# A spectral mixer gated with attention: first weights loaded in two halves on two queues, other warm-up products, and a later slot for one set of reciprocals

## The chip, the cores and the metric

The kernel runs on one core of a Trainium2 chip. A core has five instruction queues that run side by side: TensorE (PE), VectorE (DVE), ScalarE (ACT), GpSimd (POOL) and SyncE (SP), which here only issues DMA transfers. PE multiplies from SBUF into PSUM, which has eight banks of 128 x 512 fp32. The metric is device time in microseconds of one execution, as the median of several runs.

## What is computed

Two branches share the input x (2048 tokens, 512 channels, fp32), and a gate for each token mixes them.

```python
g = sigmoid((x * gate_w).sum(-1, keepdims=True))
a = einsum("ts,bse->bte", dft_seq_re, x @ dft_hid_re.T) - einsum("ts,bse->bte", dft_seq_im, x @ dft_hid_im.T)
q, k, v = split(x @ wqkv)                 # 32 heads of 16
b = (softmax(q @ k.T * 16 ** -0.5) @ v) @ wo
out = g * a + (1 - g) * b
```

## The kernel before, in words

Every fp32 operand of a large product is split into a high and a low part (fp32r); three products (high x high, high x low, low x high) accumulate in one PSUM bank.

**The start.** `staged_first` (lines 103 to 108) loads the first two tiles of 256 KB, x from ACT's queue and the first weights from SP's. `warm_up` (143 to 155) clears a tile of zeros with two memsets on DVE, then gives PE four products of 128 x 128 and seven of 128 x 512 on the zeros while the loads are under way. The fourth small product releases the other loads (line 97). `split_first` (127 to 141) casts both halves of the weights on ACT (line 136) and x on DVE (137), and then forms the low parts. The first real products are those of line 220: for each 128 rows of the contraction they need the high part of x and, product by product, one quarter of the columns of the weights.

**The main loop.** The attention walks through 512 units: 16 pairs of heads, two halves of the queries, 16 tiles of keys. For each unit PE computes scores (line 740), ACT takes the exponential (741), and PE multiplies with the values (762, in the last 16 units 748); the values carry a column of ones, so that each softmax sum comes out beside its output. Ahead of that run products whose only use is the row maxima (262); DVE reduces them (264). When the maxima of half a pair are complete, DVE, POOL and DVE turn them into rows (273, 276 and 277, 281), and DMAs place these rows beside the queries (287), where the scores pick them up. The Fourier part and the projection with `wo` (429) are woven in between by a pattern written out by hand (`segment`, `pairs`). `run_plan(u)` sets off, at the start of a slot, all steps with a due unit u; the engines then take what they got in the order of the program.

**Outputs of the attention.** The results of each half of the queries (hf 0 or 1) and of each group of four pairs (ct 0 to 3) go to DRAM. `sums` (line 531) loads the softmax sums from there as a 128 x 64 tile, `inverse` takes the reciprocals on DVE (536) and writes them to DRAM (539), and `load_o` reads outputs (554) and reciprocals, repeated for 16 rows (556), into tiles of one shape, which are multiplied and split for the projection. The last group of the second half (hf 1, ct 3) has only three pairs, so its transfers go pair by pair, six and six, and its tile is cleared first on POOL (547). Its steps are those of `last_block`: at unit 486 load outputs and reciprocals together, at 490 multiply on POOL (592), at 494 split on DVE (578, 579) into `o_lno` and `o_lnh`. Its sums are loaded at 482 and inverted at 484. For the first half (hf 0, ct 3) the same steps come later, at 498 to 506, with a step "sums" of its own for the reciprocals.

**The last 20 units.** From unit 492 on, two units make one slot: four scores, some products of the projection (line 429, dealt out by the table `whole`), four scores, sixteen products with the values. `third` is the projection of the second half's last group; its first three products stand in the slot of unit 496 and read `o_lno`. `last` is the projection of the first half's last group, in the slots 508 and 510; its banks rotate through the pools psS, psA, psD (the list `three`). psS and psA have three banks each and are shared with the scores; psD has one. The projections' banks are read out on DVE (615).

The tile framework gives each DMA of SP and ACT one of eight semaphores in turn, so a DMA also waits until the one eight places before it has landed.

Of the kernel before, what the change touches and what calls it, by code (L numbers as in the profile page):

```python
# [9 lines left out]
F32 = mybir.dt.float32  # L10
# [5 lines left out]
P = 128  # L16
S = 2048
D = 512
# [13 lines left out]
def mix_kernel(ctx: ExitStack, tc: tile.TileContext, xa_t, xa, wqkv, w_hid, w_seq, wo, gate_w, out):  # L32
# [5 lines left out]
    nc = tc.nc  # L38
# [64 lines left out]
    def staged_first(w, x):  # L103

        w_raw, x_raw = (st1.tile([P, D], F32, name="raw", bufs=RAW) for _ in range(2))
        nc.scalar.dma_start(x_raw, x)
        nc.sync.dma_start(w_raw, w)
        return w_raw, x_raw

    def add(hi, lo, src, lo_eng, shape=None):  # L110
# [16 lines left out]
    def split_first():  # L127

        (wh0, wl0, w, _, _), (xh0, xl0, x, _, _) = todo.pop(0), todo.pop(0)
        w_raw, x_raw = staged_first(w, x)  # L130
        behind.append(warm_up())
        load_ahead(RAW - 3)
        x_raw = x_raw.rearrange("p (s t) -> p s t", s=4)
        halves = [slice(i * D // 2, (i + 1) * D // 2) for i in range(2)]
        for cols in halves:
            nc.scalar.copy(wh0[:, cols], w_raw[:, cols])
        nc.vector.tensor_copy(xh0, x_raw)
        for cols in halves:
            nc.vector.tensor_tensor(wl0[:, cols], w_raw[:, cols], wh0[:, cols].bitcast(F32), ALU.subtract)
        nc.vector.tensor_tensor(xl0, x_raw, xh0.bitcast(F32), ALU.subtract)  # L140
        load_ahead()

    def warm_up():

        zeros = xab[3][:, 0, 0]
        nc.vector.memset(zeros[:, :P].bitcast(F32), 0.0)
        nc.vector.memset(zeros[:, P:].bitcast(F32), 0.0)
        make_identity(nc, ident)
        nc.vector.tensor_tensor(pairsum, ident[:, :64], ident[:, 64:], ALU.add)
        ps = psD.tile([P, 512], F32, name="d")  # L150
        for i in range(4):
            first = nc.tensor.matmul(ps[:, :P], zeros[:, :P], zeros[:, :P], start=True, stop=True)
        for i in range(7):
            nc.tensor.matmul(ps, zeros[:, :P], zeros, start=True, stop=True)
        return first

    def add_x(tb, kt):
        x = xab[tb][:, :, :, kt * P:(kt + 1) * P]
# [4 lines left out]
    def bank():  # L163
        nonlocal banks
        banks += 1
        return (psS if banks % 2 else psA).tile([P, 512], F32, name="s" if banks % 2 else "a")


    with tc.tile_pool(name="qk", bufs=1, reuse_waits="tile") as pool:
# [38 lines left out]
        for tb in range(4):  # L208
# [4 lines left out]
            for c in range(2):  # L213
                if tb == 0 and c == 0:
                    pss = [bank() for _ in range(4)]
                    for kt in range(KT):
                        x = xab[tb][:, :, :, kt * P:(kt + 1) * P]
                        for i, (w, v) in enumerate(((wh, 0), (wl, 0), (wh, 1))):
                            for ct in range(4):
                                nc.tensor.matmul(pss[ct], w[:, c, kt, ct * P:(ct + 1) * P], x[:, :, v],  # L220
                                                 start=kt == 0 and i == 0, stop=kt == KT - 1 and i == 2)
# [4 lines left out]
                for ct in range(4):  # L226
                    ps = bank()
# [143 lines left out]
    for s in range(8):  # L371
        ps = psS.tile([P, 512], F32, name="s")
# [128 lines left out]
    def place(i, dt, name):  # L501

        return const.tile([P, 2, 2, 2 * D], dt, name=name, tag=f"xab{i}")

    def tiles(t):
        return [[t[:, v, q * P:(q + 1) * P] for v in range(2)] for q in range(t.shape[2] // P)]
# [34 lines left out]
    def load_o(o, sm, hf, ct, q0, n=4):  # L541

        size = (sm if o is None else o).shape[1]
        cols = slice(q0, q0 + size)
        for t in (o, sm):
            if n < 4 and t is not None:
                nc.gpsimd.memset(t, 0.0)
        for h in range(2):
            o0 = 33 if h else 0
            for p in [slice(0, 4)] if n == 4 else [slice(i, i + 1) for i in range(n)]:  # L550
                r = slice(64 * h, 64 * h + 64) if n == 4 else slice(64 * h + p.start, 64 * h + 64, 4)
                rows = o_d[hf][4 * ct + p.start:4 * ct + p.stop, o0:o0 + 16, cols]
                if o is not None:
                    nc.sync.dma_start(o[r], rows.rearrange("p d f -> d p f"))
                if sm is not None:
                    nc.sync.dma_start(sm[r], r_d[hf][ct][h:h + 1, p, cols].broadcast_to([16, p.stop - p.start, size]))
# [20 lines left out]
    def parts(hi, lo, src):  # L577
        nc.vector.tensor_copy(hi, src)
        nc.vector.tensor_tensor(lo, src, hi.bitcast(F32), ALU.subtract)

    def last_block(step, hf, n, eng):

        if step == 0:
            if not last_o:
                last_o.append(place(1, F32, "o_raw"))
            t = last_o[0][:, hf]
            load_o(t[:, 0], t[:, 1] if hf else None, hf, 3, 0, n)
        elif step == "sums":
            load_o(None, last_o[0][:, hf, 1], hf, 3, 0, n)
        elif step == 1:  # L590
            t = last_o[0][:, hf]
            eng.tensor_tensor(t[:, 0], t[:, 0], t[:, 1], ALU.mult)
        else:
            o = last_o[0][:, hf, 0]
            if hf:
                ts = [work.tile([P, 2, D], F32R, name=f"o_l{x}", tag=x) for x in ("no", "nh")]
                for i, t in enumerate(ts):
                    parts(t[:, 0], t[:, 1], o[:, i * D:(i + 1) * D])
                oh[hf, 3] = tiles(ts[0]) + tiles(ts[1])
            else:  # L600
                t = place(2, F32R, "o_l")[:, 0]
                parts(t[:, 0], t[:, 1], o)
                oh[hf, 3] = tiles(t)
# [13 lines left out]
    def proj(hf, cts, pools, qts=range(8)):  # L617

        for qt in qts:
            t = hf * 8 + qt  # L620
            chain = Chain(*pools[qt % len(pools)], 3 * len(cts))
            for ct in cts:
                h1, l1 = oh[hf, ct][qt]
                for i, (st, mv) in enumerate(((h1, 0), (h1, 1), (l1, 0))):
                    last = ct == cts[-1] and i == 2
                    yield chain, st, wos[0][:, mv, ct], partial(proj_next, hf, cts, t, chain) if last else None
# [174 lines left out]
    def at(u, f, *args):  # L801
        plan.setdefault(u, []).append(partial(f, *args))

    for hf in range(2):
        for ct in range(4):
            n = 3 if hf and ct == 3 else 4
            last = 32 * (4 * ct + n - 1) + 16 * (hf + 1)
            at(last + (4 if ct < 3 else 2), sums, hf, ct, n)
            at(last + (12 if ct < 3 else 4), inverse, hf, ct, n)
            if ct < 3:  # L810
                for half in range(2):
                    for step, du in enumerate((16, 20, 22)):
                        at(last + du + 8 * half, block, step, hf, ct, half)
# [3 lines left out]
    one, two, three = [(psD, "d")], [(psS, "s"), (psD, "d")], [(psS, "s"), (psA, "a"), (psD, "d")]  # L817
    at(456, load_yg, 0, range(3))
    at(481, load_yg, 0, range(3, 8))
    for step, u in enumerate((486, 490, 494)):  # L820
        at(u, last_block, step, 1, 3, nc.gpsimd)
    for step, u in ((0, 498), ("sums", 500), (1, 504), (2, 506)):
        at(u, last_block, step, 0, 4, nc.gpsimd)
    at(498, load_w15)
    lead = a_next

# [75 lines left out]
    first = proj(0, (0, 1, 2), one * 5 + two[:1] + one, range(7))  # L902
# [22 lines left out]
    run_deferred()  # L925
    assert not any(a_left.values())
    third = proj(1, (3,), two)
    last = proj(0, (3,), three, range(7))

    early, late = proj(0, (0,), one, (7,)), proj(0, (1, 2, 3), [(psS, "s")], (7,))  # L930
    whole = {492: ((first, 9),), 494: ((first, 6),), 496: ((first, 3), (third, 3)), 498: ((third, 6),), 500: ((third, 6),),
# [55 lines left out]
```

## Time and profile before

| | |
|---|---|
| median of 3 runs | 1707.89 us (1707.83 to 1707.91) |
| the profiled execution | 1708.24 us, of which its span from the first to the last instruction is 1706.4 us |
| granted TensorE clock, mean | 0.999 |
| PE busy | 1698.9 us in 13042 matmuls |
| DVE busy | 1353.1 us (79%) |
| ACT busy | 1152.2 us (68%) |
| POOL busy | 450.1 us (26%) |
| DMA | 165.09 MB, 97 GB/s on average |

A row of the timeline has the start in microseconds from the first instruction, the busy time, the engine, the line of the kernel, the operation, the tile written and the tiles read, the shape, and how many instructions were merged into the row. In square brackets stands how long the engine had been idle before it, and what ended that. SPq and ACTq are the queues that issue DMAs; their time is that of issuing, not of the transfer. A row of the waits has the engine, tile and line that waited, what it waited for, the sum in microseconds, the number of waits and the longest. A row of the stage table has the stretch, its length, then PE, weight loads, DVE, ACT and POOL with busy time and number of instructions, the granted clock, the DMA engines' share and GB/s.

### The profile page before, as it was taken

What the parts mean: (1) busy time and instruction counts of PE and PEld (TensorE: products, weight loads), DVE (VectorE), ACT (ScalarE), POOL (GpSimd) and SP (SyncE); (2) the same over time, 40 slices, a digit from 0 to 9 for tenths busy, and PEclk for the clock granted to TensorE, in tenths of its full rate; (3) what the DMA queues carried; (4) which work ended last, traced back from release to release, by engine and by line L of the source; (5) the groups of instructions that cost most, each with busy time, mean ns of one, the idle gap of its engine ahead of it and who ended that gap; (6) DMA issues with size and microseconds to landing.
All of it is one profiled execution on the core that took longest, in us unless ns stands there. A gap on an engine that the chain in (4) does not pass through costs nothing.

```text
span 1706.4 us, 33519 instructions
## 1 busy us (share of the span) xinstructions
PE 1698.9 (100%) x13042; PEld 1048.2 (61%) x13042; DVE 1353.1 (79%) x2290; ACT 1152.2 (68%) x2266; POOL 450.1 (26%) x554
## 2 busy tenths in 40 slices
PE   9999999999999999999999999999999999999998
PEld 7888755556666666666666666666666666655444
DVE  5439888888888888888888888888888888889854
ACT  5212377777667777666777677776667777678886
POOL 0201121323222333222222343322323343211110
PEclk9999999999999999999999999999999999999999
DMA  9963500314141524314156535224141535362114
GB/s 289 348 143 137 153 8 17 44 36 75 57 81 40 104 81 101 69 38 81 39 94 242 101 101 109 67 63 76 51 81 57 122 104 102 131 183 42 38 29 137
DMA packets 82129, 165.09 MB, mean 97 GB/s; under 512 B 19444, under 2 KB 19682, under 8 KB 78130
## 3 DMA queue, kind: packets, MB, share of 16 engines
q1 hardware_dynamic: 77874, 162.12, 37.5%
q8 instruction: 103, 1.69, 0.4%
q0 software_dynamic: 3808, 0.30, 0.2%
q14 instruction: 56, 0.46, 0.1%
q10 hardware_dynamic: 288, 0.52, 0.1%
HBM read 107.73 MB, written 54.52 MB: 95 GB/s over the span
## 4 chain that ended last, share of the span: by engine, by line
PE 99%; DMA 0%; DVE 0%; ACT 0%; DVEq 0%; issue 0%
PE d L429 37%; PE acc L762 27%; PE a L262 11%; PE s L740 11%; PE s L343 3%; PE s L375 1%; PE d L343 1%; PE acc L748 1%; PE a L82 1%; PE a L81 1%; PE s L82 1%; PE s L81 1%; PE a L80 1%; PE s L80 1%; PE s L429 1%; PE a L429 0%
## 5 line engine op out<-in xcount | busy, mean ns | idle before, releaser
L264 DVE TENSOR_REDUCE mx<-a 128x1 f32<-128x512 f32 x2026 | 1241.0, 683 | 246.4 <-PE a L262 229.6
L741 ACT ACTIVATE pt<-s 128x512 f32<-128x512 f32 x2006 | 1022.5, 621 | 368.1 <-PE s L740 330.5
L262 PE MATMUL a<-ks,qs 48*128 48x512 f32 x2026 | 799.2, 410 | 0.0
L740 PE MATMUL s<-qs,ks 50*128 50x512 f32 x2006 | 778.3, 414 | 0.0
L429 PE MATMUL d<-xab,ch 64*128 64x512 f32 x2016 | 647.9, 396 | 0.0
L762 PE MATMUL acc<-pt,vt 128*17 128x512 f32 x3968 | 484.1, 596 | 0.0
L429 PEld LDWEIGHTS d<-xab,ch 64*128 64x128 f32 x2016 | 365.9, 184 | 126.9 <-DVE mx L264 60.4
L740 PEld LDWEIGHTS s<-qs,ks 50*128 50x128 f32 x2006 | 365.2, 184 | 84.0 <-issue 12.6
L262 PEld LDWEIGHTS a<-ks,qs 48*128 48x128 f32 x2026 | 368.9, 185 | 50.4 <-DVE mx L264 23.6
L429 PE MATMUL d<-xab,cl 64*128 64x512 f32 x1008 | 399.4, 396 | 0.0
L429 PEld LDWEIGHTS d<-xab,cl 64*128 64x128 f32 x1008 | 185.4, 184 | 65.4 <-DVE mx L264 40.8
L413 POOL CAST ch<-craw 128x512 fp32r<-128x512 f32 x126 | 77.1, 612 | 557.5 <-PE a L262 188.2
L762 PEld LDWEIGHTS acc<-pt,vt 128*17 128x17 f32 x3968 | 86.1, 96 | 201.3 <-issue 201.3
L414 POOL TENSOR_TENSOR cl<-craw,ch 128x512 fp32r<-128x512 f32 x126 | 162.4, 1289 | 10.2
L287 POOL DMA_DIRECT2D qs<-mt x119 | 67.0, 568 | 156.3 <-DVE mt L281 153.7
L429 PE MATMUL d<-wre,xab 64*128 64x512 f32 x336 | 90.4, 402 | 0.0
L429 PEld LDWEIGHTS d<-wre,xab 64*128 64x128 f32 x336 | 59.0, 184 | 38.3 <-issue 23.3
L429 PE MATMUL d<-wo_hl,o_hl 64*128 64x512 f32 (+1 forms) x246 | 68.1, 409 | 0.0
L429 PEld LDWEIGHTS d<-wo_hl,o_hl 64*128 64x128 f32 (+1 forms) x246 | 42.2, 184 | 29.4 <-issue 12.2
L76 ACT CAST hl<-s 128x512 fp32r<-128x512 f32 x28 | 16.1, 588 | 58.1 <-PE d L343 25.3
L446 POOL CAST xab<-y 128x512 fp32r<-128x512 f32 x16 | 9.8, 610 | 127.8 <-ACT y L445 99.6
L613 POOL TENSOR_TENSOR yp<-yp,few 128x512 f32<-128x512 f32 x12 | 15.4, 1283 | 104.6 <-ACT few L612 104.6
(170 smaller groups left out, 1003.7 us busy)
## 6 DMA issues: line engine op xcount, KB each, us to landing
craw<-w_seq SPq DMA_DIRECT2D x128, 256.0 KB
qk<-hl SPq DMA_DIRECT2D x32, 512.0 KB
qs<-qk SPq DMA_DIRECT2D x96, 128.0 KB
ks<-qk SPq DMA_DIRECT2D x96, 128.0 KB
b<-hl SPq DMA_DIRECT2D x16, 512.0 KB
xab<-b SPq DMA_DIRECT2D x16, 512.0 KB
o<-oe SPq DMA_DIRECT2D x62, 128.0 KB
oh<-nh SPq DMA_DIRECT2D x12, 512.0 KB
```

The costliest lines, as they stand in the source:

```text
L80: nc.tensor.matmul(ps, sh, mh, start=first, stop=False)
L81: nc.tensor.matmul(ps, sh, ml, start=False, stop=False)
L262: nc.tensor.matmul(ps, qs[p % 2][r, qt * P:(qt + 1) * P], ks[p % 2][r, kb * 512:(kb + 1) * 512], start=True, stop=True)
L264: user = nc.vector.tensor_reduce(mx[p % 2][:, h, qt, kb:kb + 1], ps, AX.X, ALU.max)
L287: (nc.gpsimd if own else nc.sync).dma_start(rows.rearrange("v (q b c) -> v b q c", q=8, b=4)[:, b], mt[hf][32 * b + h:32 * b + 32:2])
L343: i = nc.tensor.matmul(ps, st[r], mv[r], start=not half and not j, stop=half == 1 and j == 11)
L413: nc.gpsimd.tensor_copy(h1, raw)
L414: nc.gpsimd.tensor_tensor(l1, raw, h1.bitcast(F32), ALU.subtract)
L429: i = nc.tensor.matmul(self.ps, st[r], mv[r], start=not self.begun, stop=stop)
L740: nc.tensor.matmul(ps, ks[p % 2][rr, kt * P:(kt + 1) * P], qs[p % 2][rr, q0:q0 + 512], start=True, stop=True)
L741: return nc.scalar.activation(pts[u][:, 2 * qb + h], ps, AF.Exp, bias=0.0, scale=DH ** -0.5)
L762: nc.tensor.matmul(acc[32 * j:32 * j + 17], vt[:, kt, p, 16 * h:16 * h + 17], pt[:, j], start=kt == 0, stop=kt == NT - 1)
```

## The change

The first weights come in two transfers of half the columns, the first from SP's queue and the second from ACT's, behind x. Nine zero products of full width take the place of four small and seven full ones; their moving operand is one zero column repeated 512 times, so the second memset is gone, and the second product now releases the other loads. The reciprocals of the second half's last group are taken at unit 490 in place of 484; its outputs are still loaded at 486, but the reciprocals are read back in a step of their own at 492, and multiply and split both stand at 494, the multiply on DVE in place of POOL. The banks of `last` rotate through psA, psD, psS.

```diff
         nc.scalar.dma_start(x_raw, x)
-        nc.sync.dma_start(w_raw, w)
+        nc.sync.dma_start(w_raw[:, :D // 2], w[:, :D // 2])
+        nc.scalar.dma_start(w_raw[:, D // 2:], w[:, D // 2:])
...
         nc.vector.memset(zeros[:, :P].bitcast(F32), 0.0)
-        nc.vector.memset(zeros[:, P:].bitcast(F32), 0.0)
...
-        for i in range(4):
-            first = nc.tensor.matmul(ps[:, :P], zeros[:, :P], zeros[:, :P], start=True, stop=True)
-        for i in range(7):
-            nc.tensor.matmul(ps, zeros[:, :P], zeros, start=True, stop=True)
-        return first
+        row = zeros[:, :1].broadcast_to([P, 512])
+        return [nc.tensor.matmul(ps, zeros[:, :P], row, start=True, stop=True) for i in range(9)][1]
...
-            load_o(t[:, 0], t[:, 1] if hf else None, hf, 3, 0, n)
+            load_o(t[:, 0], None, hf, 3, 0, n)
...
-            at(last + (12 if ct < 3 else 4), inverse, hf, ct, n)
+            at(last + (12 if ct < 3 else 10 if hf else 4), inverse, hf, ct, n)
...
-    for step, u in enumerate((486, 490, 494)):
-        at(u, last_block, step, 1, 3, nc.gpsimd)
-    for step, u in ((0, 498), ("sums", 500), (1, 504), (2, 506)):
-        at(u, last_block, step, 0, 4, nc.gpsimd)
+    for hf, n, eng, us in ((1, 3, nc.vector, (486, 492, 494, 494)), (0, 4, nc.gpsimd, (498, 500, 504, 506))):
+        for step, u in zip((0, "sums", 1, 2), us):
+            at(u, last_block, step, hf, n, eng)
...
-    last = proj(0, (3,), three, range(7))
+    last = proj(0, (3,), three[1:] + three[:1], range(7))
```

On SP the order around the last group becomes: six L554 (outputs), two L539 (reciprocals to DRAM), eight L287 (rows of maxima), six L556 (reciprocals back). Before it was two L539, L554 and L556 in turn six times, eight L287. On DVE the reciprocal moves from among the maxima to behind the last L273, and the multiply stands ahead of L578.

## Prediction

> **What bounds the kernel now.** The page comes first, then the table of waits for PE alone.
>
> ```profile
> span 1706.4 us, 33519 instructions
> ...
> PE 1698.9 (100%) x13042; PEld 1048.2 (61%) x13042; DVE 1353.1 (79%) x2290; ACT 1152.2 (68%) x2266; POOL 450.1 (26%) x554
> ...
> PE 99%; DMA 0%; DVE 0%; ACT 0%; DVEq 0%; issue 0%
> ```
>
> ```profile
> PE d L152 <- DVE xab L146: 1.1, 1, 1.1
> PE s L429 <- ACT pt L741: 0.5, 1, 0.5
> PE s L220 <- ACT wh L136: 0.3, 1, 0.3
> ```
>
> The third line of the page is the chain that ended last: 99% of it is TensorE. The waits of PE that the profile names come to 1.9 us in three places. PE takes its matmuls in the order written, so the change is worth what it takes from, or adds to, the time at which PE reaches its next matmul. It touches that in four places: the start, one reciprocal at 1625.8, the last block of the second half at 1643 to 1655, and one PSUM bank at 1682. All between them keeps its instructions, their order on every engine, and (the one DMA more stands at the very start) which earlier DMA each later one waits for; I cost it at nothing.
>
> **The start.** The timeline from 0 to 10 us:
>
> ```profile
> 1.97 3.29 PE L154 MATMUL d<-xab 128*128 128x512 f32 x7
> ...
> 4.90 0.43 DVE L137 CAST xab<-raw 128x512 fp32r<-128x512 f32 x1 [3.33 <-DMA raw<-xa_t]
> 5.09 0.71 ACT L136 CAST wh<-raw 128x256 fp32r<-128x256 f32 x2 [2.63 <-DMA raw<-wqkv]
> ...
> 5.54 0.79 PE L220 MATMUL s<-xab,wh 128*128 128x512 f32 x1 [0.28 <-ACT wh L136]
> ...
> 6.56 0.57 PE L220 MATMUL s<-xab,wh 128*128 128x512 f32 x1
> ...
> 6.97 0.40 PE L220 MATMUL a<-xab,wh 128*128 128x512 f32 x1
> ...
> 7.20 0.40 PE L220 MATMUL s<-xab,wl 128*128 128x512 f32 x1
> ...
> 7.65 0.62 ACT L76 CAST xab<-raw 128x512 fp32r<-128x512 f32 x1
> ...
> 9.03 0.39 PE L220 MATMUL s<-xab,wh 128*128 128x512 f32 x1
> ```
>
> The first real matmul needs x in its high part (cast from 4.90, 0.43 long) and the first half of the weights (cast from 5.09, half of 0.71); it starts at 5.54. Until the second of these casts, two transfers of 256 KB share the DMA engines, 512 KB in all. After the change SP brings 128 KB of weights while ACT brings x, and the other 128 KB of weights stand behind x in ACT's queue: 128 KB fewer are in front of what the first matmul needs. The stage table gives the rate:
>
> ```profile
> 3.00:4.00 1.00, 1.00 (x4) 0.81 (x3) 0.00 (x0) 0.00 (x0) 0.00 (x0) 1.00 0.80 272
> ```
>
> 128 KB at the 272 GB/s of its last column are 0.48 us: x can be cast from about 4.45, and the first matmul can start near 5.05 (bounds: 5.54 if nothing lands sooner, 4.8 where the zero products let it in). Those don't stand in the way. At the slow pace of 0.41 us (6.56 to 6.97), nine from 1.1 make room for the next matmul at 4.8; the seven from 1.97 did so at 4.85. The memset of the other 384 columns goes from DVE, which was idle there, and what releases the next loads (now the second product, before the fourth small one) comes at about the same time, near 2.1. The second half of the weights has until the third matmul, 0.8 us after the first. The next weights and x are needed at 9.03, or 0.5 earlier, and their last high part is cast by 8.27 (7.65 plus 0.62).
>
> What 0.49 us is worth: until about 7 us a matmul comes every 0.41 us, then every 0.23 (6.97 to 7.20). If that change of pace stays where it is, the 0.49 us hold 1.2 slow matmuls, each worth 0.23 later: **-0.25 us** (bounds: 0 and -0.6). [...]
>
> **The reciprocal at 1625.8.** It leaves a stage in which DVE is nearly full of maxima.
>
> ```profile
> 1625.78 0.54 DVE L536 RECIPROCAL rc<-rc 128x64 f32<-128x64 f32 x1
> ```
>
> ```profile
> 1624.07 1.05 PE L762 MATMUL acc<-pt,vt 128*17 128x512 f32 x8
> ...
> 1627.95 1.05 PE L762 MATMUL acc<-pt,vt 128*17 128x512 f32 x8
> ...
> 1635.27 1.05 PE L762 MATMUL acc<-pt,vt 128*17 128x512 f32 x8
> ...
> 1638.88 0.62 PE L762 MATMUL acc<-pt,vt 128*17 128x512 f32 x4
> ```
>
> From one group of L762 to the next PE took 3.88 us with the reciprocal beside it, and 3.61 one round later without it. Its going is worth **-0.27 us** (bounds: 0, if that was chance, and its whole 0.54).
>
> **The last block of the second half.** Before, the reciprocals were written to DRAM (L539) and read back (six L556 between six L554) while DVE still took maxima; POOL multiplied. Now SP's sequence is: six L554, two L539 that wait for the reciprocal, eight L287 (the maxima's rows for the coming scores), six L556. DVE multiplies, then splits (L578, L579). The rows of DVE and POOL, of SP, and of PE:
>
> ```profile
> 1642.19 0.22 DVE L273 TENSOR_REDUCE nm<-mx 128x16 f32<-128x64 f32 x1
> 1643.18 0.22 POOL L277 TENSOR_TENSOR nhl<-nm,nhl 128x16 fp32r<-128x16 f32 x1
> 1643.44 0.21 DVE L281 STREAM_TRANSPOSE mt<-nhl 128x32 f32<-128x32 f32 x1 [1.02 <-DMA o_raw<-r]
> 1643.91 2.40 POOL L592 TENSOR_TENSOR o_raw<-o_raw 128x1024 f32<-128x1024 f32 x1 [0.51 <-DMA o_raw<-r]
> 1646.70 0.42 DVE L578 CAST o_lno<-o_raw 128x512 fp32r<-128x512 f32 x1
> 1647.15 0.69 DVE L579 TENSOR_TENSOR o_lno<-o_raw,o_lno 128x512 fp32r<-128x512 f32 x1
> ...
> 1678.63 1.23 DVE L579 TENSOR_TENSOR o_l<-o_raw,o_l 128x1024 fp32r<-128x1024 f32 x1
> ```
>
> ```profile
> 1626.35 1.21 SPq L539 DMA_DIRECT2D r<-rc  x2
> ...
> 1637.56 1.88 SPq L556 DMA_DIRECT2D o_raw<-r  x1
> ...
> 1640.75 0.59 SPq L554 DMA_DIRECT2D o_raw<-o  x1
> 1641.38 0.59 SPq L556 DMA_DIRECT2D o_raw<-r  x1
> 1643.68 5.37 SPq L287 DMA_DIRECT2D qs<-mt  x8
> ```
>
> ```profile
> 1653.18 0.49 PE L740 MATMUL s<-qs,ks 50*128 50x512 f32 x1
> ...
> 1653.85 0.97 PE L429 MATMUL d<-wo_hl,o_hl 128*128 128x512 f32 x3
> 1654.65 0.85 PE L429 MATMUL s<-wo_hl,o_lno 128*128 128x512 f32 x3
> 1655.43 0.49 PE L740 MATMUL s<-qs,ks 50*128 50x512 f32 x1
> ```
>
> In the clock of before: the reciprocal follows L273, 1642.41 to 1642.95. The transpose isn't later for it, since POOL's L277 ends at 1643.40 anyway. SP issues the two L539 from 1643.0 (1.21 together), the eight L287 from 1644.2 (5.37), the six L556 from 1649.6 at 0.63 each (1640.75 to 1641.38). The last starts at 1652.7. Before, POOL began 2.53 us after the last L556 was issued, so DVE's multiply begins at 1655.25. The trace has no such row on DVE; the nearest are L579 on the same shape at 1.23 and POOL's own 2.40, and I take 1.2. The high part of o_lno is then ready at about 1656.9 (0.42), the low part at 1657.6 (0.69).
>
> PE wants o_lno at 1654.65 (in the changed order its wait even stands one matmul earlier, on the last of the three at 1653.85). It stops until 1656.9, goes through four matmuls at 0.23 and reaches the next scores at 1657.95 instead of 1655.43: **+2.5 us**. Bounds: +1.9 if SP passes L539 half a microsecond sooner and DVE needs 0.1 less, +3.7 if DVE takes POOL's 2.40.
>
> What else is behind these waits: the last L287 is issued half a microsecond later than before, at 1648.9. With the 2.53 us of L556 its rows are there by 1651.4, and PE needs them at 1653.18: covered by 1.8 us; beyond that each microsecond would hold PE. POOL clears the factors' half of the tile before it is needed, between L277 and the first L556. DVE's L615, which free the banks of the two finished chains, stand behind multiply and split, to about 1658.7; PE's next use of those banks is a whole slot later. After the stop PE runs no faster, as the profile names one more wait of PE only, the bank below; so the 2.5 us last to the end.
>
> **The bank at 1682.** The first product of the last stage took a bank of psS that ACT had yet to read.
>
> ```profile
> 1682.38 0.96 PE L429 MATMUL s<-wo_hl,o_l 128*128 128x512 f32 x3 [0.45 <-ACT pt L741]
> ```
>
> ```profile
> 1680.67 0.62 ACT L741 ACTIVATE pt<-a 128x512 f32<-128x512 f32 x1
> 1681.73 0.60 ACT L741 ACTIVATE pt<-s 128x512 f32<-128x512 f32 x1 [0.44 <-PE a L740]
> ```
>
> It came free at 1682.33, the end of ACT's row at 1681.73. With the pools turned to a, d, s the first chain takes a bank that is free from 1681.29, the end of ACT's row at 1680.67, before PE is there; the s bank is needed third, six matmuls later. **-0.5 us** (bounds: 0 and -0.55). The last group is turned as well; none of its banks was waited for, and I cost it at nothing.
>
> **The sum.** -0.25 - 0.27 + 2.5 - 0.5 = +1.5 us. The profiled execution took 1708.24 (its span of 1706.4 and 1.84 around it), 0.35 above the median of the runs, 1707.89. The terms are differences within it, so I add them to the median: **1709.4 us**, 0.09% slower. A measurement of this kernel can tell about 0.2%, 3.4 us, from no change.
>
> **The rivals.**
> - The split brings nothing: x and both halves land together, as transfers that share the engines may. For it: all of them keep the same engines busy. Against it: ACT's queue holds x ahead of the second half. The start gives 0: 1709.6.
> - An issue on SP is held up. One L556 took 1.88 us where its neighbours took 0.59; such a hold among the fourteen issues from 1644 to 1653 adds 1.3 us to PE's stop: 1710.7. Against it: it was one of twelve.
> - TensorE's faster pace starts later, since nine zero products stand where eleven were. A microsecond of delay costs 1 - 0.23/0.41 = 0.44 us. The slow pace lasted 6 us from the first product; half as much again costs 1.3: 1710.7. Against it: PE is busy over the same stretch. [...]
> - The other side, faster: the six L556 are out in time. SP's fourteen issues take 5.37 + 6 x 0.63 = 9.15 us in my sum; at 0.5 us each they take 7.0, the stop falls to 0.4 us, and the other edits win: 1707.3. It decides from a stop of 1.0 us, or 0.55 us an issue. Against it: L287's eight in 5.37.
>
> **How the numbers follow.** Forecast 0.62, split without effect 0.14, SP held up 0.08, late pace 0.07, L556 in time 0.05, others 0.04. The extremes of the four terms together give +0.2 and +3.7; not all of them lie at one end, so the forecast's own bounds are +0.6 to +2.7. The range takes in the first three rivals and leaves out the fast one: 1708.3 to 1711.0. More than 3.4 us slower needs two dear cases together, or DVE's multiply at POOL's price with one of them: 0.07. More than 3.4 us faster has no mechanism here: 0.02. Between: 0.91.
>
> **What would show it.** In the changed kernel: the first L220 near 5.05; about 3.6 us between the two groups of L762 that were 3.88 apart; L592 on DVE, starting some 2.5 us after the last L556, and those behind eight L287; in PE's table of waits one for DVE's L578 of some 2.5 us, the largest there; none for ACT at the first product of the last stage. I am wrong if that largest wait is missing or under 1 us, or if PE loses time where the order is unchanged.

## The result, and the profile after

The changed kernel takes **1711.32 us** (median of 17 runs, 1709.61 to 1713.02) beside 1708.02 of the kernel before (17 runs, 1707.48 to 1709.97): a ratio of 1.0019 with a 95% interval from 1.0012 to 1.0025. That is 3.3 us more, where 1.5 was forecast. The runs don't spread evenly: five lie at 1709.6 to 1710.0 with a mean granted clock of 0.999 to 1.000, eight at 1711.0 to 1711.7 with 0.998, four at 1712.6 to 1713.0 with 0.997. The profiled execution, at 1709.82, is one of the first five. In the changed kernel a line behind 155 has a number three lower than before (L426 for L429, L737 for L740, and so on).

Its page (span, and the chain that ended last) and its table of waits for PE:

```profile
span 1708.0 us, 33511 instructions
...
PE 99%; SPq 1%; DVE 0%; DMA 0%; issue 0%; DVEq 0%
```

```profile
PE s L426 <- DVE o_lno L575: 2.1, 1, 2.1
PE d L152 <- DVE xab L147: 1.1, 1, 1.1
```

The waits for ACT and for the first weights are gone; one of 2.1 us for `o_lno` has come. Where it comes from is in the timelines of SP, of DVE and of PE:

```profile
1642.09 1.21 SPq L536 DMA_DIRECT2D r<-rc  x2
1643.41 5.31 SPq L284 DMA_DIRECT2D qs<-mt  x8
1648.82 3.69 SPq L553 DMA_DIRECT2D o_raw<-r  x6
```

```profile
1654.23 1.23 DVE L589 TENSOR_TENSOR o_raw<-o_raw 128x1024 f32<-128x1024 f32 x1 [8.27 <-DMA o_raw<-r]
1655.56 0.43 DVE L575 CAST o_lno<-o_raw 128x512 fp32r<-128x512 f32 x1
```

```profile
5.18 0.79 PE L217 MATMUL s<-xab,wh 128*128 128x512 f32 x1
...
1623.55 1.05 PE L759 MATMUL acc<-pt,vt 128*17 128x512 f32 x8
...
1627.15 1.05 PE L759 MATMUL acc<-pt,vt 128*17 128x512 f32 x8
...
1653.02 0.97 PE L426 MATMUL d<-wo_hl,o_hl 128*128 128x512 f32 x3
1656.13 1.13 PE L426 MATMUL s<-wo_hl,o_lno 128*128 128x512 f32 x3 [2.15 <-DVE o_lno L575]
1657.19 0.50 PE L737 MATMUL s<-qs,ks 50*128 50x512 f32 x1
...
1657.86 1.91 PE L759 MATMUL acc<-pt,vt 128*17 128x512 f32 x16
1659.70 0.50 PE L737 MATMUL s<-qs,ks 50*128 50x512 f32 x1
...
1683.62 0.97 PE L426 MATMUL a<-wo_hl,o_l 128*128 128x512 f32 x3
```

SP issues eight L284 before the six L553, as forecast; DVE multiplies 1.7 us after the last issue has ended (1652.51), and PE stands for 2.15 us. The groups of L759 are 3.60 us apart in place of 3.88, and the last stage begins without a wait. In this execution every step is there, and it is 1.6 us longer than the profiled execution before. What the other runs add is not in this profile.

### The profile page after: what moved, and what is told of

It is laid out like the page before. It is cut to its first block, busy times and chain, and to the rows that moved or that the text cites. A ratio compares the mean times of both kernels' runs of the same rounds, so it can differ in the third digit from the quotient of the medians.

```text
span 1708.0 us, 33511 instructions
## 1 busy us (share of the span) xinstructions
PE 1698.7 (99%) x13040; PEld 1049.5 (61%) x13040; DVE 1353.8 (79%) x2290; ACT 1152.1 (67%) x2266; POOL 447.6 (26%) x553
## 4 chain that ended last, share of the span: by engine, by line
PE 99%; SPq 1%; DVE 0%; DMA 0%; issue 0%; DVEq 0%
PE d L426 36%; PE acc L759 27%; PE a L259 11%; PE s L737 11%; PE s L340 3%; PE s L372 1%; PE d L340 1%; PE acc L745 1%; PE a L82 1%; PE a L80 1%; PE s L82 1%; PE s L80 1%; PE a L81 1%; PE s L81 1%; PE a L426 0%; PE s L426 0%
## 5 line engine op out<-in xcount | busy, mean ns | idle before, releaser
L737 PE MATMUL s<-qs,ks 50*128 50x512 f32 x2006 | 778.6, 414 | 0.0
L426 PE MATMUL d<-xab,ch 64*128 64x512 f32 x2016 | 648.0, 396 | 0.0
L759 PE MATMUL acc<-pt,vt 128*17 128x512 f32 x3968 | 484.1, 596 | 0.0
L426 PEld LDWEIGHTS d<-xab,ch 64*128 64x128 f32 x2016 | 366.0, 184 | 126.2 <-DVE mx L261 60.4
L737 PEld LDWEIGHTS s<-qs,ks 50*128 50x128 f32 x2006 | 365.2, 184 | 84.3 <-issue 12.8
L426 PE MATMUL d<-xab,cl 64*128 64x512 f32 x1008 | 399.4, 396 | 0.0
L426 PEld LDWEIGHTS d<-xab,cl 64*128 64x128 f32 x1008 | 185.4, 184 | 65.0 <-DVE mx L261 40.8
L759 PEld LDWEIGHTS acc<-pt,vt 128*17 128x17 f32 x3968 | 86.1, 96 | 201.2 <-issue 201.2
L284 POOL DMA_DIRECT2D qs<-mt x119 | 67.0, 568 | 156.2 <-DVE mt L278 153.6
L426 PE MATMUL d<-wre,xab 64*128 64x512 f32 x336 | 90.5, 402 | 0.0
L426 PEld LDWEIGHTS d<-wre,xab 64*128 64x128 f32 x336 | 59.0, 184 | 38.4 <-issue 23.3
L426 PE MATMUL d<-wo_hl,o_hl 64*128 64x512 f32 (+1 forms) x246 | 68.2, 409 | 0.0
L426 PEld LDWEIGHTS d<-wo_hl,o_hl 64*128 64x128 f32 (+1 forms) x246 | 42.2, 184 | 29.5 <-issue 12.2
```

What stands on the lines that cost most here:

```text
L284: (nc.gpsimd if own else nc.sync).dma_start(rows.rearrange("v (q b c) -> v b q c", q=8, b=4)[:, b], mt[hf][32 * b + h:32 * b + 32:2])
L426: i = nc.tensor.matmul(self.ps, st[r], mv[r], start=not self.begun, stop=stop)
L737: nc.tensor.matmul(ps, ks[p % 2][rr, kt * P:(kt + 1) * P], qs[p % 2][rr, q0:q0 + 512], start=True, stop=True)
L759: nc.tensor.matmul(acc[32 * j:32 * j + 17], vt[:, kt, p, 16 * h:16 * h + 17], pt[:, j], start=kt == 0, stop=kt == NT - 1)
```

## The experiments

The profiled execution shows 1.6 us of the loss; twelve of the 17 runs take 1.2 to 3.2 us more than it. Two theories for that rest. **Theory A:** after its stop for `o_lno` TensorE loses its clock for a while, in most runs. **Theory B:** the new zero products leave it slow for longer at the start. Later a **theory C** was added: the stop pushes scores, exponentials and read-outs into each other.

**The parts alone.** The first four ran on one chip, where the kernel before took 1708.15 us (33 runs).

```diff
# r1_start: only the edits of staged_first and warm_up
+        nc.scalar.dma_start(w_raw[:, D // 2:], w[:, D // 2:])
...
# r2_late: only those of last_block, inverse and their slots
+            at(last + (12 if ct < 3 else 10 if hf else 4), inverse, hf, ct, n)
...
# r3_bank: only the rotation of the banks
+    last = proj(0, (3,), three[1:] + three[:1], range(7))
# r4_after: all of it
```

> Only the start is changed (weights in two transfers on two queues, nine zero products of full width). Theory A, the clock is lost at PE's stop near 1654: there is no stop here, so the time is 0.2 to 0.4 us below before, its runs lie within 1 us of each other, and the clock is that of before. Theory B, the new zero products leave TensorE slow for longer at the start in most runs: 1.0 to 1.5 us above before at the median, with runs spread over 3 us.

> Only the last block of the second half is changed (reciprocals at 490, read back at 492, multiply on DVE at 494); start and banks as before. Both theories: a wait of PE for DVE's o_lno of about 2.2 us, and 0.27 us less at the reciprocal. Theory A: 3.5 to 4.5 us above before at the median, runs spread over 3 us, clock below 0.999 in most of them. Theory B: 2.0 to 2.4 us above before, runs within 1 us of each other.

> Only the banks of the last projection rotate as psA, psD, psS. Both theories: 0.5 us below before, no wait of PE for ACT at the first product of the last stage, runs as close together as those of before.

> The whole change once more. Both theories: about 1711.3 at the median with runs from 1709.6 to 1713. If its profile falls on a run over 1711, theory A wants a stretch of slow matmuls (0.4 us apart in place of 0.23) that begins within 4 us of PE's stop near 1654; theory B wants it before 12 us. If the spread was of that chip alone, the runs lie within 1 us of 1709.8.

The start alone: 1708.13 us, ratio 1.0000 (0.9991 to 1.0009). The last block alone: 1711.73, 1.0021 (1.0012 to 1.0030). The bank alone: 1707.46, 0.9997 (0.9989 to 1.0006). All of it: 1711.58, 1.0019 (1.0010 to 1.0028), two of eleven runs at 1710.1 and nine at 1711.3 to 1711.9. B falls: the loss is in the last block. One sign of A did not come: it had foretold runs spread over 3 us for r2_late, and they lie between 1711.08 and 1712.47. The profile of r2_late has a row and stretches that the other profiles so far lack; the first is from the timeline of PE, the others from the stage table (the granted clock is the third figure from the end):

```profile
1656.94 1.14 PE L429 MATMUL s<-wo_hl,o_lno 128*128 128x512 f32 x3 [2.37 <-DVE o_lno L578]
...
1658.67 3.55 PE L762 MATMUL acc<-pt,vt 128*17 128x512 f32 x16
```

```profile
1657.00:1658.00 1.00, 1.00 (x3) 0.40 (x3) 0.97 (x3) 0.00 (x0) 0.00 (x0) 1.00 0.00 0
1658.00:1659.00 1.00, 1.00 (x9) 0.45 (x12) 1.00 (x2) 0.46 (x1) 0.00 (x0) 0.81 0.07 16
1659.00:1660.00 1.00, 1.00 (x8) 0.17 (x4) 0.91 (x2) 1.00 (x4) 0.00 (x0) 0.50 0.03 8
...
1662.00:1663.00 1.00, 1.00 (x9) 0.48 (x6) 0.00 (x0) 0.70 (x2) 0.00 (x0) 0.98 0.00 0
```

Sixteen products with the values take 3.55 us where they take 1.91 in the changed kernel's profile, and for that time the granted clock is 0.50.

**The stop with PE kept busy, without a stop, and longer.** The next four shared a chip and the kernel before at 1708.01 us (28 runs).

```diff
# r5_busy, in the slot of unit 496, ahead of the first product of `third`
+                        bank.ps = bank.pool.tile([P, 512], F32, name=bank.name)
+                        for _ in range(9):
+                            nc.tensor.matmul(bank.ps, oh[1, 2][7][0], wos[0][:, 0, 2], start=True, stop=True)
...
# r6_queue, load_o called by the step "sums"
-                    nc.sync.dma_start(sm[r], r_d[hf][ct][h:h + 1, p, cols].broadcast_to([16, p.stop - p.start, size]))
+                    eng.dma_start(sm[r], r_d[hf][ct][h:h + 1, p, cols].broadcast_to([16, p.stop - p.start, size]))
...
+            load_o(None, last_o[0][:, hf, 1], hf, 3, 0, n, nc.gpsimd if hf else nc.sync)
...
# r7_later, the table `whole`
-    whole = {492: ((first, 9),), 494: ((first, 6),), 496: ((first, 3), (third, 3)), 498: ((third, 6),), 500: ((third, 6),),
-             502: ((third, 3),), 504: ((early, 3), (third, 3)), 506: ((third, 3),), 508: ((last, 9),), 510: ((last, 12),)}
+    whole = {492: ((first, 9),), 494: ((first, 6),), 496: ((first, 3),), 498: ((third, 6),), 500: ((third, 6),),
+             502: ((third, 6),), 504: ((early, 3), (third, 3)), 506: ((third, 3),), 508: ((last, 9),), 510: ((last, 12),)}
...
# r8_pool
-    for hf, n, eng, us in ((1, 3, nc.vector, (486, 492, 494, 494)), (0, 4, nc.gpsimd, (498, 500, 504, 506))):
+    for hf, n, eng, us in ((1, 3, nc.gpsimd, (486, 492, 494, 494)), (0, 4, nc.gpsimd, (498, 500, 504, 506))):
```

> The whole change, with nine products of full size (results overwritten, so nothing of the output changes) put into TensorE's order just where it stops for o_lno; each takes 0.23 us, 2.1 us in all, so TensorE works through most of the time that it would stand idle, and the next wanted product comes no earlier. Theory A (the clock is lost after the stop because TensorE stands idle): the stop of about 2.1 us remains as cost, the half-speed stretch behind it does not come: 1709.6 to 1710.2, all runs within 0.8 us of each other, and no stretch in the profile under full clock after 1654 us. Rival C (the extra microsecond and more comes of what stands behind the stop: scores, exponentials and divisions pushed into each other): nothing changes, 1711.3 to 1711.9, or more.

> The whole change, with the six loads of the reciprocals for the second half's last block issued by POOL instead of SP, so that they no longer stand behind the eight loads of the maxima's rows. They can be issued from about 1646 us, two us after the store, and the multiplication can start 2.5 us after the last of them, near 1651.5 if POOL issues one in 0.6 us; o_lno is then there at 1653.2, before TensorE asks for it at 1654. Theory A: no stop, no loss of the clock; what is left of the change is the reciprocal (-0.27) and the bank (-0.7): 1707.1 to 1707.5. Rival C gives the same here, since there is no stop. If POOL's issues take over 1 us each, part of the stop stays.

> The whole change, with the three products of the first chain that uses o_lno taken from the slot at 1654 us and three more put into the slot six units later; the same products in all. o_lno is wanted some 3 us later, near 1657.5, and is ready at 1657. Theory A: stop of under 0.5 us, no loss of the clock: 1707.0 to 1708.0. Against that stands the emptied slot, in which TensorE may wait for ACT's exponentials: up to 0.7 us (three products of 0.23) more. Rival C: the same. A result above 1709 would mean that the emptied slot stops TensorE as long as o_lno did.

> The whole change, but POOL multiplies in place of DVE, 2.40 us instead of 1.23 by the rows shown: the stop grows by 1.2 us, to about 3.3. Theory A: the stop's cost grows by 1.2 and every run loses the clock for one stretch of 3.4 us or two (1.6 us each), so 1712.5 to 1714.5, with no run under 1711.5. Rival C (cost follows the stop alone, the extra is fixed): 1712.5 to 1713.1.

r5_busy: 1709.80 us, all eleven runs between 1709.53 and 1710.05, ratio 1.0010 (1.0001 to 1.0019). Its timeline of PE:

```profile
1654.16 2.23 PE L939 MATMUL s<-wo_hl,o_hl 128*128 128x512 f32 x9
1656.23 1.21 PE L426 MATMUL s<-wo_hl,o_lno 128*128 128x512 f32 x3
...
1658.04 1.91 PE L759 MATMUL acc<-pt,vt 128*17 128x512 f32 x16
```

The wanted product comes as late as in the changed kernel, and all that stands behind it is as late; only PE isn't idle, and the granted clock is 1.00 from 1654 to 1662 us. The upper groups of times are gone, and C with them: the 1.5 to 1.8 us beyond 1709.8 belong to the idle time, not to the delay.

r6_queue: 1707.42 us (1706.83 to 1708.01), ratio 0.9997 (0.9988 to 1.0006). POOL, DVE and PE:

```profile
1644.62 2.94 POOL L553 DMA_DIRECT2D o_raw<-r  x6 [0.92 <-DMA r<-rc]
```

```profile
1649.69 1.22 DVE L589 TENSOR_TENSOR o_raw<-o_raw 128x1024 f32<-128x1024 f32 x1 [3.52 <-DMA qs<-mt]
```

```profile
1653.23 0.97 PE L426 MATMUL d<-wo_hl,o_hl 128*128 128x512 f32 x3
1654.03 0.85 PE L426 MATMUL s<-wo_hl,o_lno 128*128 128x512 f32 x3
1654.82 0.49 PE L737 MATMUL s<-qs,ks 50*128 50x512 f32 x1
```

Moved off SP, the six loads are issued while SP is still busy with the maxima's rows, and the stop is gone. From the first of these rows to the scores PE takes 1.59 us; in the changed kernel it takes 4.17 (1653.02 to 1657.19). The stop costs 2.58 us by the trace and 2.38 by the medians of r5 and r6.

r7_later: 1708.08 us, ratio 1.0001 (0.9992 to 1.0009). No stop for `o_lno` and no group above 1708.7; but it is 0.66 us above r6. Its profile names three waits that r6 lacks: two for x at the start, which is the same in both kernels (0.6 us, below, and 0.2), and in the slot behind the emptied one 0.3 us for a bank that DVE reads out late. So of these only the last can come of the edit; the first and the last:

```profile
PE s L217 <- ACT xab L76: 0.6, 1, 0.6
PE d L426 <- DVE yp_qs L612: 0.3, 1, 0.3
```

r8_pool: 1712.86 us (six runs, 1712.05 to 1713.88), ratio 1.0028 (1.0016 to 1.0039): none under 1711.5, as A said. Its waits of PE and its row of the sixteen products:

```profile
PE s L426 <- DVE o_lno L575: 3.1, 1, 3.1
```

```profile
1659.45 3.40 PE L759 MATMUL acc<-pt,vt 128*17 128x512 f32 x16
```

**Shorter stops.** Two runs with fewer fillers, `range(4)` and `range(2)` in place of `range(9)`; the kernel before took 1708.12 us beside these and the two after them.

> The whole change with four filler products (results overwritten) in the stop instead of nine: 0.92 us of it is filled, about 1.2 us stay idle. The times of the whole change so far fall apart: 7 of 28 lie at 1709.6 to 1710.2, as with nine fillers, the rest 1.2 us and more above. [...] Rival: any stop of a microsecond can cost the clock: some of the runs lie near 1711.3.

> The same with two fillers, 0.46 us: about 1.65 us stay idle. [...]

r9_fill4: 1710.08 us, ratio 1.0010 (1.0001 to 1.0019); ten runs at 1709.5 to 1710.2 and one at 1711.09, whose mean clock of 1.000 shows no loss. r10_fill2: 1711.30, 1.0015 (1.0006 to 1.0024); five runs at 1709.6 to 1710.4, six at 1711.3 to 1712.3. The stops in their profiles, r9's first:

```profile
PE s L426 <- DVE o_lno L575: 1.0, 1, 1.0
```

```profile
PE s L426 <- DVE o_lno L575: 1.4, 1, 1.4
```

By the times, the clock was lost in 0 of 11 runs at 1.0 us idle, in 6 of 11 at 1.4, in 22 of 29 at 2.0 to 2.15 (the whole change), and in all six at 3.1 (r8). Those of r2, at 2.4, don't part into groups. Two limits of these counts: the idle times are those of one profiled execution each, and r10's, at 1.4, is one of the five runs without loss; and a time alone doesn't prove that the clock was lost, since the kernel before has runs some 2 us above its others too (five of 27 beside r13 to r15, at a mean clock of 0.999 to 1.000; their cause is not known).

**The whole change seen losing it.** Up to here no profile of the changed kernel itself showed the loss.

> The whole change, one profiled run. If it takes 1711 to 1712 us, the clock's record has one stretch of 3.41 us at half the clock, beginning 0 to 3.5 us after TensorE resumes, and the sixteen products of that slot take 3.4 to 3.6 us instead of 1.91. If it takes under 1710.2, there is none, as in the two profiles so far. If it takes 1712.6 or more, there are two such stretches, or a stop of over 3 us, or another loss that none of the profiles has shown yet.

This run took 1711.39 us. Its waits, timeline of PE and stage table:

```profile
PE s L426 <- DVE o_lno L575: 2.0, 1, 2.0
...
PE s L217 <- ACT xab L76: 0.5, 1, 0.5
```

```profile
1655.98 1.14 PE L426 MATMUL s<-wo_hl,o_lno 128*128 128x512 f32 x3 [1.96 <-DVE o_lno L575]
...
1657.71 3.60 PE L759 MATMUL acc<-pt,vt 128*17 128x512 f32 x16
1661.25 0.49 PE L737 MATMUL s<-qs,ks 50*128 50x512 f32 x1
```

```profile
1657.00:1658.00 1.00, 1.00 (x9) 0.44 (x12) 1.00 (x2) 0.42 (x1) 0.00 (x0) 0.89 0.00 0
1658.00:1659.00 1.00, 1.00 (x8) 0.19 (x4) 0.94 (x2) 1.00 (x3) 0.00 (x0) 0.50 0.06 16
1659.00:1660.00 1.00, 1.00 (x8) 0.19 (x4) 0.00 (x0) 0.64 (x2) 0.00 (x0) 0.50 0.00 0
1660.00:1661.00 1.00, 1.00 (x8) 0.00 (x0) 0.00 (x0) 0.00 (x0) 0.00 (x0) 0.50 0.00 0
1661.00:1662.00 1.00, 1.00 (x9) 0.39 (x5) 0.00 (x0) 0.64 (x2) 0.00 (x0) 0.90 0.00 0
```

The clock 0.89 and 0.90 in the outer stretches puts half speed from 1657.78 (0.22 us at 0.5) to 1661.20: 3.42 us. PE had resumed 1.8 us before it falls. From the sixteen products to the next scores it takes 3.54 us against 1.84 in the profile without the loss (1657.86 to 1659.70): **1.70 us**. The means of the two groups lie 1.4 us apart in the first 17 runs, 1.5 in r4 and 1.8 in r10.

**Where the start's gain went.** In r1_start the first real product came 0.48 us earlier than in the profile before, and the time was the same. The last issue on ACT stands at the same distance from the last product in all kernels, but not from the end of the span. The kernel before, r1_start and the changed kernel, with spans of 1706.4, 1706.9 and 1708.0 us:

```profile
1702.83 0.38 ACTq L702 DMA_DIRECT2D out<-yp  x1
```

```profile
5.06 0.73 PE L217 MATMUL s<-xab,wh 128*128 128x512 f32 x1
...
8.11 0.62 ACT L76 CAST xab<-raw 128x512 fp32r<-128x512 f32 x1 [0.29 <-DMA raw<-xa_t]
...
8.79 0.50 PE L217 MATMUL s<-xab,wh 128*128 128x512 f32 x1
...
1702.96 0.38 ACTq L699 DMA_DIRECT2D out<-yp  x1
```

```profile
1704.06 0.38 ACTq L699 DMA_DIRECT2D out<-yp  x1
```

From the last issue to the end that is 3.57 us before and 3.94 in both kernels with the edits of the start; the spans are given to 0.1 us, so such lengths hold to 0.05.

The longer end is not all of it. In the profile of r1_start (1708.73 us, the longest of its eleven runs) the next x is cast at 8.11 us, where it was cast at 7.65 before, and the product that waits for it comes at 8.79, where it came at 9.03: half of the lead of 0.48 us is gone there. The last issue on ACT even stands 0.13 us later than before. In the profile of the changed kernel the lead lasts (the group of L759 at 1623.55 stood at 1624.07 before), and there the longer end takes most of it back.

By the author's reading of the built program, which no profile shows, SP ends by waiting for the eight semaphores of the queues one after the other; the last store has the last of them before, and the first of them when one transfer was added ahead of it. r11 leaves the split out; r12 does so in the version without the stop; r13, r14 and r15 move other loads to POOL until the last store has the last semaphore again (for the last three the kernel before took 1707.62).

```diff
# r11_zero: of the change only the zero products
# r12_best: r6_queue, with the first weights in one transfer
+        nc.sync.dma_start(w_raw, w)
# r13_startq: r1_start; r14_best2: r6_queue; in both
-                nc.sync.dma_start(gwb, gate_w.broadcast_to([P, D]))
+                nc.gpsimd.dma_start(gwb, gate_w.broadcast_to([P, D]))
# r14_best2 and r15_best3 (this from r12_best)
+            load_o(None, last_o[0][:, hf, 1], hf, 3, 0, n, nc.gpsimd)
```

> The kernel before with the new zero products alone, nine of full width from one column, and the weights in one transfer. With the three edits of the start together, the profiles show the first product 0.4 us earlier and the stretch from the last store's issue on ACT to the end of the span 0.35 us longer (3.92 to 3.94 against 3.57 to 3.61), and the time unchanged. If the longer end comes with the added transfer on ACT's queue, it is 3.57 to 3.61 here, and the time 1707.8 to 1708.3: neither the gain of the start nor its loss. If it comes with the zero products, it is 3.93 here and the time about 1708.4.

> The whole change with the reciprocals' loads issued by POOL (1707.42, no stop) and with the first weights in one transfer again. If the added transfer costs 0.35 us at the end and gains about as much at the start, this is 1707.2 to 1707.6, the same as with the split within what can be told; if the split gained nothing at the start, 1707.0 to 1707.1. A stretch of 3.57 to 3.61 us from the last store's issue to the end is expected either way; 3.9 would put that loss on another edit.

> The three edits of the start alone, and the one load of the gate's weights (early in the kernel, far from the end) issued by POOL instead of SP: so many transfers on the hardware queues as before, and the last store has the last of the eight semaphores for which SP waits in turn at the end. If an earlier place in that row costs the end 0.35 us: from the last store's issue on ACT to the end of the span 3.57 to 3.65 us, and the start's gain of 0.25 to 0.35 us shows, 1707.7 to 1707.9 beside 1708.1 before. If the added transfer itself prolongs the end: 3.93 and 1708.1 as in the run of the start alone.

> The whole change with the reciprocals' loads of both last blocks and the load of the gate's weights issued by POOL: eight transfers fewer on the hardware queues, so the last store has the last semaphore again, and no stop of TensorE. By the theory of the semaphores' order: 3.57 to 3.65 us at the end, 0.35 less than the same kernel with an earlier semaphore (1707.42): 1707.0 to 1707.2, -0.9 to -1.1 beside before. Without it 1707.4.

> As the run with the loads of the reciprocals on POOL and the first weights in one transfer (1707.64), but with those of both last blocks on POOL, eight fewer on the hardware queues: last semaphore again. By the theory 3.57 to 3.65 us at the end and 1707.2 to 1707.4; without it 1707.6 again. The split is worth the difference to the run beside it: 0.1 to 0.3 us if it gains at the start what the profiles show.

| | us | ratio, interval | last issue to the end, us |
|---|---|---|---|
| r11_zero | 1707.96 | 0.9999 (0.9990 to 1.0007) | 3.65 |
| r12_best | 1707.64 | 0.9996 (0.9987 to 1.0005) | 3.91 |
| r13_startq | 1707.62 | 0.9998 (0.9989 to 1.0008) | 3.63 |
| r14_best2 | 1707.96 | 0.9999 (0.9991 to 1.0008) | 4.48 |
| r15_best3 | 1706.97 | 0.9994 (0.9986 to 1.0003) | 3.80 |

r12 takes the blame from the split as such: 3.91 us without it, the last store with an early semaphore. r13 has the short end that the order of the semaphores foretold, but the gain of 0.25 to 0.35 us does not show in its median; r14 has the last semaphore and the longest end, and r15, with the last one too, has 3.80, above the 3.57 to 3.65 foretold. So the end grew in the changed kernel by 0.37 us, that is seen; that the order of the semaphores does it is supported by r12 and r13, contradicted by r14, not borne out by r15, and stays open.

r15 is the best version: 0.65 us under the kernel before in the medians, where the changed kernel is 3.3 to 3.4 above it. Like r3 and r6 it can't be told from the kernel before by its interval.

## Why the prediction was wrong, point by point

- **The start, -0.25:** its first part held: the first product came at 5.18 us in the profile after and at 5.06 in r1, forecast 5.05. (By the prediction's own figures the term is 1.2 x 0.23 = 0.28.) The time moved by 0.0. Two steps failed. The next x is not "cast by 8.27", a time taken over from the profile before: in r1 its cast ends at 8.73, and PE waits for it (in r16 0.5 us). And what follows the start was costed at nothing, but the end of the span grew by 0.37 us in the kernels with the edits of the start; the cause of that stays open.
- **The reciprocal, -0.27:** right, 3.60 us for 3.88 (-0.28).
- **The stop, +2.5:** right in its size and its working. The last six issues took 3.69 us (forecast 3.78), the multiplication 1.23 (1.2), and the stop cost 2.58. One sum is loose: four products of 0.23 from 1656.9 end at 1657.8, not 1657.95, so the working gives +2.4; PE took 1.06 us from `o_lno` to the next scores (1656.13 to 1657.19).
- **"After the stop PE runs no faster, ... so the 2.5 us last to the end":** this step failed. The term was read as time that PE lacks, and nothing was added for what the idle time does to the pace behind it. In the run of the changed kernel whose profile shows it (r16) PE then ran at half clock for 3.42 us, which cost 1.70 us more; by their times 22 of 29 runs paid this. I had a rival with a slower pace, but only at the start, and called PE busy there; I did not ask the same of the stop that I forecast myself. In r16 1.96 us of idle time came ahead of the loss.
- **The bank, -0.5:** right by the trace. From the sixteen products to the first product of the last stage PE takes 2.51 us in r3 and 3.03 before (1679.35 to 1682.38, the row in the prediction); in the medians r3 gained 0.69. The row before, then those of r3:

```profile
1679.35 1.91 PE L748 MATMUL acc<-pt,vt 128*17 128x512 f32 x16
```

```profile
1679.97 1.91 PE L748 MATMUL acc<-pt,vt 128*17 128x512 f32 x16
...
1682.48 0.96 PE L429 MATMUL a<-wo_hl,o_l 128*128 128x512 f32 x3
```

With the measured terms the sum is 0 - 0.28 + 2.58 - 0.52 = +1.8 us; r5, in which PE isn't idle, has +1.79. With 1.70 for the clock it is +3.5; the median is +3.3. The likeliest case of the forecast is thus what a quarter of the runs did.

Four of the first 17 runs, at 1712.6 to 1713.0 us, lie 1.3 us higher still. Their mean clock of 0.997 would fit a second stretch at half speed; no profile caught one, so this stays open.

## What to carry to other kernels

The stop of TensorE had two prices here: its own length (2.58 us), and the clock behind it (1.70 us in r16). Where a change adds a wait such as these (1.4 us in r10's profile, 1.96 in r16) to an engine that was busy before, price both, and look whether the runs fall into groups, as r10's did. If the wait can't be removed, try filler products: with them the clock stayed at 1.00 (r5, 1709.80 us). Better is to look which queue holds the transfer back, and whether an idle engine can issue it (r6, 1707.42 us).

## What the runs showed of the hardware

- In the profiles that show the loss the clock fell not at the stop but after PE had resumed: 1.8 us in r16 and 1.7 in r2; in r8 the scores that start 1.4 us after it are the first slow ones (0.53 us for 0.39).
- The granted clock was then 0.50, for 3.42 us in r16 (1657.78 to 1661.20) and for 3.42 us in r2 (1658.62 to 1662.04, from 0.81 and 0.98 in the outer stretches), and 1.00 again behind it (r16 from 1662, r2 from 1663), with PE busy all through the stretch.
- The length of the stop alone did not decide whether the clock fell: it was 2.15 us in the changed kernel's first profile and 1.98 in r4's, at a granted clock of 1.00 from 1652 to 1666 us and from 1652 to 1670, and 1.96 in r16, which lost it. What else decides was not shown.
- From the last issue on ACT to the end of the program it took 3.57 us (the kernel before) to 4.48 us (r14) in kernels whose last work is the same.
